# One attention and expert kernel: k in tiles of four blocks, with the scores at a tile's first block as two products

## The chip, the cores and the metric

The kernel runs on one core of one Trainium2 chip. What counts is the time of one execution on the device, in microseconds (us). Each kernel is run several times; the median is shown, with the lowest and the highest. One more execution is taken with the hardware profiler, and all rows come from it.

## What is computed

Windowed attention over 8 batches, 8 heads, 576 positions and a head size of 64, in f32, and behind it a mixture of 8 experts with one expert for each token. The output of the attention, (4608, 512), is the tokens of the second part. The change lies in the scores of the first part.

```python
scores = scale * np.matmul(q, k.transpose(0, 1, 3, 2))
rel = pos[:, None] - pos[None, :]
mask = (rel >= 0) & (rel < window)            # window = 64
scores = np.where(mask, scores, -1000000000.0)
attn = np.exp(scores - max); attn = attn / (sum(attn) + 1e-09)
out = np.matmul(attn, v)
...
do_compute = (x @ w_skip) > 0; e_idx = argmax(xc @ w_gate)
h = np.maximum(xc[mask] @ w1[e], 0.0)
y[mask] = gate_w[mask, None] * (h @ w2[e]);  out[do_compute] = xc + y
```

A position sees itself and the 63 before it. With blocks of 64 positions (9 for each batch), a block of queries therefore needs two blocks of keys: its own and the one before it.

## The kernel before

**Tiles.** A tile is 128 tokens: two blocks of 64, one in each half of the partitions. `token_tiles` gives 36 of them in four rounds m of 9: four tiles for each of the two batches of a round (blocks 0 to 7), and a tail tile, r = 8, with block 8 of both batches. PE's array is used in four parts of 64x64: hf, the half of the tile (which block), picks the columns and r, one of two heads, the rows. p runs over the four pairs of heads.

**Loads.** q, k and v come in groups n = 2b + g of four blocks (g is the half of a batch, NG = 16). `load_qk` (L203) loads q and k of a group, `load_v` (L309) vT and vm of it: vT feeds the gate's product (`gate`, L332, product pw at L336), vm the product av (L388). `load_qk_tail` (L213) and `load_v_tail` load block 8 for a round. k has four fixed tiles of five blocks, `ks` (L198): slot 0 of a tile is a copy of the block before the tile's first. For a first half (g = 0) there is none, and slot 0 of the tiles 0 and 2 is set to zero once, by two memsets on POOL (L200). For a second half (g = 1) the load takes five blocks of kT, the last of the first half among them. A tail load takes two blocks of each batch's kT, 7 and 8. So every window of two blocks of keys lies side by side, and `windows` (L222) gives each half of a tile one piece of 128 columns.

**Scores.** `score(t)` (L231) writes the mask into the PSUM tile ps with four products of 512 columns (the band, L238), and adds 16 products of q with 128 columns of k (L252). The mask has -2^36 in every masked place; for block 0 the whole first half is masked. Then DVE subtracts the row maximum, ACT takes the exponent, PE transposes (pt, L285), ACT copies, PE multiplies with v (av, L388), DVE divides, and SP stores.

**Order.** All is written by hand under `tc.manual_schedule()`: each engine's queue has the order of the code. In iteration t of the loop at L1144 come the loads that are due (`at`: q and k five tiles ahead of their first use, v four), then score(t + 1), gate products, softmax of t, av of t - 2, the transposes of t - 1. The loads stand on SP's queue, only the first ones also on ACT's. SP's transfers use eight semaphores in turn (DMAHW0 to 7): each waits until the transfer eight before it has landed, beside what its own buffer needs. A pool gives out the buffer that came free first.

After tile 35 come the last routing steps and the experts, whose weights SP loads from L833 on. Neither is touched.

Of the kernel before, what the change touches and what calls it, by code (L numbers as in the profile page):

```python
# [8 lines left out]
F32 = mybir.dt.float32  # L9
# [11 lines left out]
P = 128  # L21
# [24 lines left out]
LAT = 320  # L46
ROUND = 1.5 * 2.0**23

NQB, NKB, NVB, NTB, NSB, NPB, XPB = 4, 4, 4, 2, 2, 3, 4

AHEADQ, AHEADV = 5, 4
SDELAY = 2
# [21 lines left out]
def token_tiles():  # L74
    tiles = []
    for b in range(B):
        for j in range(4):
            tiles.append(((b, 2 * j), (b, 2 * j + 1)))
        if b % 2 == 1:
            tiles.append(((b - 1, 8), (b, 8)))  # L80
    return tiles
# [62 lines left out]
def window_attention_moe(ctx: ExitStack, tc, a, out):  # L144
    nc = tc.nc
    tiles = token_tiles()
# [47 lines left out]
    qkp = scoring.enter_context(tc.tile_pool(name="qkp", bufs=1))  # L194


    NG = 2 * B
    ks = [qkp.tile([P, 5, 4, 64], F32, name=f"k{s}") for s in range(NKB)]  # L198
    for k in ks[::2]:
        nc.gpsimd.memset(k[:, 0], 0.0)  # L200
    qs, tails = {}, {}

    def load_qk(n, parts=((0, 4),), other=nc.sync):  # L203
        b, g = divmod(n, 2)
        if parts[0][0] == 0:
            qs[n] = qkp.tile([P, 4, 4, 64], F32, name="q", bufs=NQB)
        q, k = qs[n], ks[n % NKB]
        for s, e in parts:
            s0 = s + 1 if s or not g else 0
            nc.sync.dma_start(k[:, s0 : e + 1], a["kT"][b, :, 4 * g + s0 - 1 : 4 * g + e])  # L210
            other.dma_start(q[:, s:e], a["qT"][b, :, 4 * g + s : 4 * g + e])

    def load_qk_tail(m):  # L213

        q = qkp.tile([P, 2, 4, 64], F32, name="qt")
        k = qkp.tile([P, 2, 2, 4, 64], F32, name="kt")
        for z in range(2):
            nc.sync.dma_start(k[:, z], a["kT"][2 * m + z, :, 7:9])
            nc.sync.dma_start(q[:, z], a["qT"][2 * m + z, :, 8])
        tails[m] = q, k  # L220

    def windows(t):  # L222

        m, r = divmod(t, 9)
        if r == 8:
            q, k = tails[m]
            return [(q[:, z], k[:, z]) for z in range(2)]
        n, j = 4 * m + r // 2, 2 * (r % 2)
        return [(qs[n][:, j + z], ks[n % NKB][:, j + z : j + z + 2]) for z in range(2)]

    def score(t):  # L231

        ps = psc.tile([P, 2, 4, P], F32, name="ps")
        kinds = [min(i, 1) for _, i in tiles[t]]
        for hf in range(2):
            for r in range(2):
                h = slice(64 * r, 64 * r + 64)
                nc.tensor.matmul(  # L238
                    ps[64 * hf : 64 * hf + 64, r],
                    identb[h, h],  # L240
                    band[h, kinds[hf]].unsqueeze(1).to_broadcast([64, 4, P]),
                    start=True,
                    stop=False,
                    skip_group_check=True,
                )
        win = windows(t)
        for p in range(4):
            for hf in range(2):
                for r in range(2):
                    h = slice(64 * r, 64 * r + 64)  # L250
                    q, k = win[hf]
                    nc.tensor.matmul(  # L252
                        ps[64 * hf : 64 * hf + 64, r, p],
                        q[h, p],
                        k[h, :, p],
                        start=False,
                        stop=p == 3,
                        skip_group_check=True,
                    )
        ss[t] = ps  # L260

    def soften(t):
# [841 lines left out]
    with tc.manual_schedule():  # L1104
        other = nc.scalar
        nc.sync.dma_start(identb, a["c_identb"])
        other.dma_start(band, a["c_band"])
        load_qk(0, ((0, 1),), other)
        load_qk(0, ((1, 2),), other)
        load_qk(0, ((2, 4),), other)  # L1110
        load_vT(0)
        other.dma_start(wg, a["wg"])
# [6 lines left out]
        at = {}  # L1119
# [16 lines left out]
        for m in range(B // 2):  # L1136
            when_at(9 * m + 4, load_qk_tail, m)
            when_at(9 * m + 2, load_v_tail, m)
            lower_at.setdefault(9 * m + 4, []).append((tail_lower, m, 0))
            lower_at.setdefault(9 * m + 7, []).append((tail_lower, m, 1))  # L1140
            gate_at.setdefault(9 * m + 5, []).append((gate_tail, m))
            gate_at.setdefault(9 * m + 6, []).append((gate_tail_t, m))
        score(0)
        for t in range(NT - 1):  # L1144
            m, r = divmod(t, 9)
            for f, n in at.get(t, ()):
                f(n)
            score(t + 1)
            gates = gate_at.get(t, ())
            if t > 1:  # L1150
# [200 lines left out]
        while True:  # L1351
            k = place[0]
            i, qi = steps[min(k, len(steps) - 1)]
# [14 lines left out]
    with tc.For_i(0, more, 1) as i:  # L1368
# [3 lines left out]
        at = mr.tile([P, NT], I32, name="atl")  # L1372
# [11 lines left out]
        for qi in range(NQ):  # L1384
            both = []
            for w in range(2):
                n = 2 * qi + w
# [56 lines left out]
```

## Time and profile before

| | us |
|---|---|
| median of 3 runs | 423.96 |
| lowest, highest | 423.83, 426.25 |
| the profiled execution's time | 421.13 |
| its span in the trace | 419.4 |
| PE busy | 397.0 |
| DVE busy | 292.0 |
| ACT busy | 220.1 |
| POOL busy | 159.3 |

The trace is that of the profiled execution alone, so rows are held against its 421.13 us, and what is worked out there is carried over to the median. PE is TensorE's products, PEld its weight loads, DVE VectorE, ACT ScalarE, POOL GpSimd, SP the queue that issues most transfers. An f32 product of the program is two rows of the profile. Busy time of PE counts from a product's start to its modelled end, and products overlap: where a row gives a stretch and a count, the time from its start to the start of the next row is what it took of PE.

### The profile page before, as it was taken

Reading aid. Unit: us, or ns where it says so; the run is one execution under the profiler, and the core shown is the slowest. Engines: PE = TensorE matmul, PEld = TensorE weight load, DVE = VectorE, ACT = ScalarE, POOL = GpSimd, SP = SyncE. Lnnn points to the kernel's source line nnn. Section 1 sums busy time; section 2 is a strip of 40 time slices with the busy share of each in tenths; the row PEclk is TensorE's granted clock in tenths of the full one; section 3 lists DMA queues with packets and bytes.
Section 4 is the critical chain, followed back from the end, with each engine's and each line's share of the span. In section 5 each row is a group of like instructions: output and inputs, shape, how many; then the busy total and the mean of one; then the engine's idle time right before and its main releaser. Section 6 shows DMA issues by size and latency. Waiting matters only on the chain.

```text
span 419.4 us, 11769 instructions
## 1 busy us (share of the span) xinstructions
PE 397.0 (95%) x4673; PEld 333.4 (80%) x4673; DVE 292.0 (70%) x513; ACT 220.1 (52%) x388; POOL 159.3 (38%) x298
## 2 busy tenths in 40 slices
PE   5998999999999989889999999999999999999992
PEld 3666878888778778679988898898888889988881
DVE  2596799989799797999437679555556485656561
ACT  0775777777767685536224436234335345544530
POOL 5211148756958878576203105013016030101011
PEclk9999899999999999999999999999999999999997
DMA  8999999999996596546928937545388765767800
GB/s 264 406 339 337 402 379 346 408 413 310 364 412 228 148 357 215 185 160 184 333 72 274 304 121 246 193 157 204 129 269 267 263 203 193 239 196 233 280 33 21
DMA packets 38840, 105.71 MB, mean 252 GB/s; under 512 B 4896, under 2 KB 6816, under 8 KB 38784
## 3 DMA queue, kind: packets, MB, share of 16 engines
q1 hardware_dynamic: 34160, 93.51, 65.2%
q0 software_dynamic: 3200, 9.58, 6.5%
q10 hardware_dynamic: 1424, 1.85, 1.2%
q8 instruction: 37, 0.61, 0.6%
q14 instruction: 19, 0.16, 0.1%
HBM read 90.86 MB, written 14.39 MB: 251 GB/s over the span
## 4 chain that ended last, share of the span: by engine, by line
PE 73%; DMA 9%; DVE 6%; POOL 5%; ACT 3%; issue 2%; ACTq 0%; DVEq 0%; POOLq 0%
PE p L910 9%; PE p L912 8%; PE p L911 8%; PE av L388 6%; PE pt L285 5%; PE ps L252 4%; PE yv L910 4%; PE yv L911 4%; PE yv L912 4%; DMA vTt<-vTt 3%; PE yw L910 3%; PE yw L912 3%; PE yw L911 3%; DMA k<-kT 2%; PE px L887 2%
## 5 line engine op out<-in xcount | busy, mean ns | idle before, releaser
L846 DVE TENSOR_TENSOR wlo<-raw,whi 128x1024 fp32r<-128x1024 f32 x70 | 86.9, 1253 | 17.5 <-ACT whi L842 17.4
L956 ACT ACTIVATE hh<-p 128x256 fp32r<-128x256 f32 (+6 forms) x72 | 27.7, 385 | 127.0 <-PE p L912 126.3
L910 PE MATMUL p<-xh,whi 128*128 128x256 f32 (+6 forms) x288 | 85.4, 296 | 0.2 <-DVE hl L959 0.2
L912 PE MATMUL p<-xh,wlo 128*128 128x256 f32 (+6 forms) x288 | 83.7, 291 | 0.6 <-DVE wlo L846 0.6
L911 PE MATMUL p<-xl,whi 128*128 128x256 f32 (+6 forms) x288 | 83.5, 290 | 0.0
L842 ACT CAST whi<-raw 128x1024 fp32r<-128x1024 f32 x72 | 74.3, 1046 | 0.1
L994 POOL DMA_INDIRECT out<-yo,les x18 | 17.6, 976 | 146.7 <-DVE yo L993 144.2
L959 DVE SCALAR_TENSOR_TENSOR hl<-p,hh 128x256 fp32r<-128x256 f32 (+6 forms) x72 | 30.2, 420 | 60.7 <-ACT hh L956 35.0
L910 PEld LDWEIGHTS p<-xh,whi 128*128 128x128 f32 x288 | 54.5, 189 | 3.8 <-issue 1.7
L911 PEld LDWEIGHTS p<-xl,whi 128*128 128x128 f32 x288 | 54.6, 190 | 1.0
L912 PEld LDWEIGHTS p<-xh,wlo 128*128 128x128 f32 x288 | 54.6, 190 | 0.8 <-DVE wlo L846 0.8
L271 DVE TENSOR_REDUCE mx<-ps 128x8 f32<-128x1024 f32 x36 | 43.6, 1212 | 9.7 <-PE ps L252 9.7
L277 ACT ACTIVATE s<-s 128x1024 f32<-128x1024 f32 x36 | 38.1, 1059 | 22.3 <-DVE s L272 22.2
L272 DVE TENSOR_TENSOR s<-ps,mx 128x1024 f32<-128x1024 f32 x36 | 44.1, 1225 | 5.0 <-ACT vm L364 0.5
L388 PEld LDWEIGHTS av<-vm,ptm 128*64 128x64 f32 x992 | 35.0, 137 | 10.9 <-issue 3.9
L388 PE MATMUL av<-vm,ptm 128*64 128x74 f32 x992 | 40.0, 232 | 2.0 <-ACT ptm L286 1.1
L286 ACT COPY ptm<-pt 128x512 f32<-128x512 f32 x72 | 38.3, 582 | 5.4 <-PE pt L285 5.4
L285 PE MATMUL pt<-ident,s 128*128 128x128 f32 x288 | 40.0, 283 | 0.0
L252 PE MATMUL ps<-k,q 64*64 64x128 f32 x1024 | 36.9, 280 | 2.6 <-DMA q<-qT 1.7
L252 PEld LDWEIGHTS ps<-k,q 64*64 64x64 f32 x1024 | 32.1, 139 | 7.0 <-issue 3.2
L285 PEld LDWEIGHTS pt<-ident,s 128*128 128x128 f32 x288 | 31.6, 143 | 2.5 <-issue 0.2
L357 POOL COPY vm<-vm 64x1184 f32<-64x1184 f32 x16 | 18.7, 1167 | 33.8 <-ACT vm L356 31.0
(224 smaller groups left out, 695.8 us busy)
## 6 DMA issues: line engine op xcount, KB each, us to landing
raw<-wq SPq DMA_DIRECT2D x72, 512.0 KB, 4.9
vm<-vp SPq DMA_DIRECT2D x15, 592.0 KB, 9.1
vT<-vT SPq DMA_DIRECT2D x16, 512.0 KB, 7.5
out<-x SPq DMA_DIRECT2D x32, 256.0 KB, 7.3
q<-qT SPq DMA_DIRECT2D x14, 512.0 KB, 8.8
wr<-wq SPq DMA_DIRECT2D x24, 256.0 KB, 5.7
k<-kT SPq DMA_DIRECT2D x7, 640.0 KB, 8.4
k<-kT SPq DMA_DIRECT2D x7, 512.0 KB, 8.5
```

The costliest lines, as they stand in the source:

```text
L252: nc.tensor.matmul(ps[64 * hf : 64 * hf + 64, r, p], q[h, p], k[h, :, p], start=False, stop=p == 3, skip_group_check=True,)
L271: nc.vector.tensor_reduce(mx, flat, axis=AX.X, op=ALU.max)
L272: pace[0] = nc.vector.tensor_tensor(s, flat, mx.unsqueeze(2).to_broadcast([P, 8, P]), op=ALU.subtract)
L277: nc.scalar.activation(s, s, AF.Exp, scale=0.125)
L285: nc.tensor.transpose(pt[:, p], s[:, 4 * r + p], ident)
L286: nc.scalar.copy(ptm[:, 4 * r : 4 * r + 4], pt)
L388: nc.tensor.matmul(av[64 * hf : 64 * hf + 64, h // 4, (h % 4) * VW : (h % 4 + 1) * VW], ptm[:, (h % 2) * 4 + h // 2, 64 * hf : 64 * hf + 6 ...
L842: nc.scalar.copy(ring[n % RING][0], raws[n % NRAW])
L846: by.tensor_tensor(lo, raws[n % NRAW], hi.bitcast(F32), op=ALU.subtract)
L910: nc.tensor.matmul(o, lh, rh, start=first, stop=False)
L911: nc.tensor.matmul(o, lh, rl, start=False, stop=False)
L912: nc.tensor.matmul(o, ll, rh, start=False, stop=last)
```

## The change

k of a group lies in a tile of four blocks of its own, from a pool with five buffers, as q's does. The block in front is not loaded again and nothing is set to zero. `windows` now answers for one half of a tile and gives pieces: for a block inside a group one piece of 128 columns, as before; for block 4 (the first of a second half) and block 8 (the tail) two pieces of 64, the first from the tile of the group before; for block 0 one piece of 64 columns, its own block. `score` runs over p, then the pieces z, then the halves, then r. A tail load takes block 8 of k for both batches, then of q.

```diff
--- before.py
+++ after.py
@@ -46,7 +46,7 @@
 LAT = 320
 ROUND = 1.5 * 2.0**23
 
-NQB, NKB, NVB, NTB, NSB, NPB, XPB = 4, 4, 4, 2, 2, 3, 4
+NQB, NKB, NVB, NTB, NSB, NPB, XPB = 4, 5, 4, 2, 2, 3, 4
 
 AHEADQ, AHEADV = 5, 4
 SDELAY = 2
@@ -195,38 +195,39 @@
 
 
     NG = 2 * B
-    ks = [qkp.tile([P, 5, 4, 64], F32, name=f"k{s}") for s in range(NKB)]
-    for k in ks[::2]:
-        nc.gpsimd.memset(k[:, 0], 0.0)
-    qs, tails = {}, {}
+    qs, ks, tails = {}, {}, {}
 
     def load_qk(n, parts=((0, 4),), other=nc.sync):
         b, g = divmod(n, 2)
         if parts[0][0] == 0:
             qs[n] = qkp.tile([P, 4, 4, 64], F32, name="q", bufs=NQB)
-        q, k = qs[n], ks[n % NKB]
+            ks[n] = qkp.tile([P, 4, 4, 64], F32, name="k", bufs=NKB)
         for s, e in parts:
-            s0 = s + 1 if s or not g else 0
-            nc.sync.dma_start(k[:, s0 : e + 1], a["kT"][b, :, 4 * g + s0 - 1 : 4 * g + e])
-            other.dma_start(q[:, s:e], a["qT"][b, :, 4 * g + s : 4 * g + e])
+            nc.sync.dma_start(ks[n][:, s:e], a["kT"][b, :, 4 * g + s : 4 * g + e])
+            other.dma_start(qs[n][:, s:e], a["qT"][b, :, 4 * g + s : 4 * g + e])
 
     def load_qk_tail(m):
 
-        q = qkp.tile([P, 2, 4, 64], F32, name="qt")
-        k = qkp.tile([P, 2, 2, 4, 64], F32, name="kt")
-        for z in range(2):
-            nc.sync.dma_start(k[:, z], a["kT"][2 * m + z, :, 7:9])
-            nc.sync.dma_start(q[:, z], a["qT"][2 * m + z, :, 8])
-        tails[m] = q, k
-
-    def windows(t):
+        tails[m] = [qkp.tile([P, 2, 4, 64], F32, name=f"{x}t") for x in "kq"]
+        for x, z in zip("kq", tails[m]):
+            for hf in range(2):
+                nc.sync.dma_start(z[:, hf], a[x + "T"][2 * m + hf, :, 8])
+
+    def windows(t, hf):
 
         m, r = divmod(t, 9)
+        b, i = tiles[t][hf]
         if r == 8:
-            q, k = tails[m]
-            return [(q[:, z], k[:, z]) for z in range(2)]
-        n, j = 4 * m + r // 2, 2 * (r % 2)
-        return [(qs[n][:, j + z], ks[n % NKB][:, j + z : j + z + 2]) for z in range(2)]
+            k, q = tails[m]
+            return q[:, hf], [(ks[2 * b + 1][:, 3:4], 0), (k[:, hf : hf + 1], 64)]
+        n, j = 2 * b + i // 4, i % 4
+        k = ks[n]
+        if j:
+            win = [(k[:, j - 1 : j + 1], 0)]
+        else:
+            win = [(ks[n - 1][:, 3:4], 0)] if i else []
+            win.append((k[:, 0:1], 64))
+        return qs[n][:, j], win
 
     def score(t):
 
@@ -243,20 +244,22 @@
                     stop=False,
                     skip_group_check=True,
                 )
-        win = windows(t)
+        win = [windows(t, hf) for hf in range(2)]
         for p in range(4):
-            for hf in range(2):
-                for r in range(2):
-                    h = slice(64 * r, 64 * r + 64)
-                    q, k = win[hf]
-                    nc.tensor.matmul(
-                        ps[64 * hf : 64 * hf + 64, r, p],
-                        q[h, p],
-                        k[h, :, p],
-                        start=False,
-                        stop=p == 3,
-                        skip_group_check=True,
-                    )
+            for z in range(2):
+                for hf in range(2):
+                    q, parts = win[hf]
+                    for k, at in parts[z : z + 1]:
+                        for r in range(2):
+                            h = slice(64 * r, 64 * r + 64)
+                            nc.tensor.matmul(
+                                ps[64 * hf : 64 * hf + 64, r, p, at : at + 64 * k.shape[1]],
+                                q[h, p],
+                                k[h, :, p],
+                                start=False,
+                                stop=p == 3,
+                                skip_group_check=True,
+                            )
         ss[t] = ps
 
     def soften(t):
```

What stands in the queues now is told by the built programs, one row for instructions of one kind that follow each other (x is their number; here a product is one instruction). PE, score(2), the tile of blocks 4 and 5 of batch 0. Before, with the band's products ahead of it:

```order
41 L238 MATMUL ps<-band,identb 64x512
42 L238 LDWEIGHTS identb
43 L238 MATMUL ps<-band,identb 64x512
44 L252 MATMUL ps<-k_107,q 64x128 x16
45 L285 MATMUL pt<-ident,s 128x128 x8
```

And with the change, at the same place:

```order
51 L255 MATMUL ps<-k,q 64x64 x2
52 L255 MATMUL ps<-k,q 64x128 x2
53 L255 MATMUL ps<-k,q 64x64 x4
54 L255 MATMUL ps<-k,q 64x128 x2
55 L255 MATMUL ps<-k,q 64x64 x4
56 L255 MATMUL ps<-k,q 64x128 x2
57 L255 MATMUL ps<-k,q 64x64 x4
58 L255 MATMUL ps<-k,q 64x128 x2
59 L255 MATMUL ps<-k,q 64x64 x2
60 L288 MATMUL pt<-ident,s 128x128 x8
```

16 products became 24: for each p two narrow ones of block 4's first piece, two wide ones of block 5, two narrow ones of block 4's second piece. The rows around it stand as before.

PE, score(8), the first tail tile. Before it was one row of 16 products as well; with the change:

```order
148 L255 MATMUL ps<-k,qt 64x64 x4
149 L255 MATMUL ps<-kt,qt 64x64 x4
150 L255 MATMUL ps<-k,qt 64x64 x4
151 L255 MATMUL ps<-kt,qt 64x64 x4
152 L255 MATMUL ps<-k,qt 64x64 x4
153 L255 MATMUL ps<-kt,qt 64x64 x4
154 L255 MATMUL ps<-k,qt 64x64 x4
155 L255 MATMUL ps<-kt,qt 64x64 x4
156 L339 MATMUL pw<-vT,wg 32x256 x4
```

16 products of 128 columns became 32 of 64, half of them on the second halves' k and half on the tail's own.

SP, from the load of k for group 4 to that of vm for group 4 (the sizes are elements for each partition). Before:

```order
21 L210 DMA k_106<-kT 128x1024
22 L211 DMA q<-qT 128x1024
23 L218 DMA kt<-kT 128x512
24 L219 DMA qt<-qT 128x256
25 L218 DMA kt<-kT 128x512
26 L219 DMA qt<-qT 128x256
27 L426 DMA out<-x 128x512
28 L296 DMA vT<-vT 128x1024
29 L302 DMA vm<-vp 128x2x592
```

With the change:

```order
20 L206 DMA k<-kT 128x1024
21 L207 DMA q<-qT 128x1024
22 L214 DMA kt<-kT 128x256 x2
23 L214 DMA qt<-qT 128x256 x2
24 L429 DMA out<-x 128x512
25 L299 DMA vT<-vT 128x1024
26 L305 DMA vm<-vp 128x2x592
```

The number of transfers is the same, so each keeps its place in the turn of eight; the two loads of kt stand together and are half as large. Everywhere else on SP only sizes differ. On POOL the two memsets of k are gone; the order of DVE and ACT is the same.

## Rows read from the trace of the kernel before

**Rows 1.** The page's first section: busy us (share of the span) x instructions.

```profile
PE 397.0 (95%) x4673; PEld 333.4 (80%) x4673; DVE 292.0 (70%) x513; ACT 220.1 (52%) x388; POOL 159.3 (38%) x298
```

**Rows 2.** The page's shares of the chain that ended last, by engine.

```profile
PE 73%; DMA 9%; DVE 6%; POOL 5%; ACT 3%; issue 2%; ACTq 0%; DVEq 0%; POOLq 0%
```

**Rows 3.** The waits of PE: engine, product, line, cause; total us, times, longest.

```profile
PE ps L252 <- DMA q<-qT: 1.7, 2, 1.2
...
PE av L388 <- POOL vm L357: 0.8, 1, 0.8
PE ps L252 <- issue: 0.8, 1, 0.8
```

**Rows 4.** The chain that ended last, in order of time: start us, us, what.

```profile
18.42 13.09 DMA vTt<-vTt
...
34.00 7.13 DMA vT<-vT
```

**Rows 5.** Timeline of PE: start us, stretch us, line, product, shape, count [wait before].

```profile
31.64 0.42 PE L336 MATMUL pw<-vTt,wg 128*32 128x128 f32 x8 [0.98 <-DMA vTt<-vTt]
...
38.35 1.04 PE L252 MATMUL ps<-kt,qt 64*64 64x128 f32 x32
41.26 0.64 PE L336 MATMUL pw<-vT,wg 128*32 128x256 f32 x8 [1.87 <-DMA vT<-vT]
41.83 1.67 PE L388 MATMUL av<-vm,ptm 128*64 128x74 f32 x32
43.43 1.97 PE L285 MATMUL pt<-ident,s 128*128 128x128 f32 x8
45.33 0.64 PE L238 MATMUL ps<-band,identb 64*64 64x512 bf16 x4
45.75 1.12 PE L252 MATMUL ps<-k,q 64*64 64x128 f32 x32
...
57.16 0.41 PE L238 MATMUL ps<-band,identb 64*64 64x512 bf16 x4
57.40 1.04 PE L252 MATMUL ps<-k,q 64*64 64x128 f32 x32
58.38 0.64 PE L336 MATMUL pw<-vT,wg 128*32 128x256 f32 x8
58.95 1.25 PE L388 MATMUL av<-vm,ptm 128*64 128x74 f32 x32
60.13 1.10 PE L285 MATMUL pt<-ident,s 128*128 128x128 f32 x8
61.16 0.41 PE L238 MATMUL ps<-band,identb 64*64 64x512 bf16 x4
```

**Rows 6.** Windows: stretch, its us, engines busy (x), granted clock, DMA share, GB/s.

```profile
31.64:41.26 9.62, 7.75 (x163) 6.43 (x164) 6.18 (x13) 5.93 (x11) 1.92 (x5) 1.00 0.98 336
39.39:41.26 1.87, 0.00 (x1) 0.03 (x1) 1.74 (x4) 0.57 (x1) 0.00 (x0) 1.00 1.05 365
42.48:45.90 3.42, 3.42 (x36) 2.75 (x35) 2.29 (x5) 1.99 (x3) 0.00 (x0) 0.50 1.01 400
45.33:57.16 11.83, 11.83 (x241) 9.48 (x240) 9.79 (x17) 8.54 (x14) 4.46 (x6) 0.98 1.03 408
```

**Rows 7.** Transfers issued up to 45 us: queue, count, KB each, median us to landing.

```profile
k<-kT SPq DMA_DIRECT2D x2, 640.0 KB, 8.8
...
kt<-kT SPq DMA_DIRECT2D x2, 256.0 KB, 6.0
```

**Rows 8.** Windows of L252 alone, inside one score: PE and PEld busy (x running).

```profile
57.40:57.42 0.02, 0.02 (x4) 0.02 (x4) 1.00 1.93 768
57.42:57.51 0.09, 0.09 (x4) 0.09 (x4) 1.00 1.06 421
57.51:57.53 0.02, 0.02 (x8) 0.02 (x8) 1.00 0.27 102
```

**Rows 9.** Timeline of PE, the end of score(0) and the start of score(1).

```profile
6.69 0.64 PE L238 MATMUL ps<-band,identb 64*64 64x512 bf16 x2
6.89 0.42 PE L252 MATMUL ps<-k,q 64*64 64x128 f32 x2
```

## The prediction

> **What bounds the kernel now.** The page's first section says which engine to follow: PE is busy for 397.0 of 419.4 us [rows 1]. The shares of the chain that ended last say the same: PE 73%, and transfers 9% [rows 2]. So something that shortens transfers can only pay inside those 9%, and something that lengthens PE pays nearly everywhere. Next the waits of PE: 1.7 us for q at the start, 0.8 us for POOL, and 0.8 us put down to "issue" [rows 3]; the two waits for v stand in the timeline of PE, 0.98 us ahead of 31.64 and 1.87 us ahead of 41.26 [rows 5]. After 41.26 PE waits for no transfer in the attention stage.
>
> The chain in order of time shows where the 9% are: 13.09 us of the load of vTt from 18.42, and 7.13 us of the load of vT (group 4) from 34.00 to 41.13 [rows 4]. The windows agree: the 16 DMA engines are at a share of 0.98 to 1.05 there, and move 336 to 408 GB/s [rows 6]. The first 41 us are thus a stream of bytes that PE waits for; from 41 us to the end of the attention stage PE runs from one product to the next, with few waits [rows 3]. A tile is then 4.00 us of PE (57.16 to 61.16), of which the scores are 0.98 us, 57.40 to 58.38 [rows 5].
>
> [...]
>
> **The change, part by part.** *Fewer bytes.* A second-half load of k falls from 640 to 512 KB, a tail load of k from 256 to 128 KB [rows 7]. Over the kernel that is 16 times 128 KB. Ahead of the vT load that PE waits for at 41.26 stand the second half of batch 0 (its first part falls from 384 to 256 KB), that of batch 1, and two tail loads: 4 x 128 KB = 0.524 MB. At 408 to 336 GB/s [rows 6] that is 1.28 to 1.56 us; I take 1.3. Half of it stands ahead of vTt, so the 0.98 us wait falls to about 0.3, PE comes to the second wait some 0.65 us sooner, and its 1.87 us fall to about 1.2. Together **-1.3 us**.
>
> *The clock.* [...] Start to start: av 41.83 to 43.43 = 1.60 against 58.95 to 60.13 = 1.18; the transposes 43.43 to 45.33 = 1.90 against 60.13 to 61.16 = 1.03; the band 45.33 to 45.75 = 0.42 against 57.16 to 57.40 = 0.24 [rows 5]. The sum of the differences is 0.42 + 0.87 + 0.18 = 1.47 us. The clock fell after a wait of 1.87 us and not after those of 0.98 and 0.8 us [rows 3, 5]. With 1.2 us to go I am nearer to the latter, and take it as gone: **-1.47 us**; the other end is 0.
>
> *More products.* Block 4 of each batch (8 tiles) has 8 products more, each tail tile (4 of them) 16; the profile shows every f32 product as two rows (16 products are its x32), so 16 and 32 rows. Block 0 has as many as before, half as wide. Tiles 2, 6 and 8 lie in front of the wait at 41.26, which hides them. 9 tiles remain: 11, 15, 20, 24, 29, 33 and the tails 17, 26, 35. The trace has no f32 product of 64 columns on a 64x64 part of the array, so its price is bounded. Far end: each row costs its share of a score, 0.98/32 = 0.031 us, whatever its columns; 6 x 16 + 3 x 32 = 192 rows are 5.9 us. Near end: only columns count. The rows speak for it: the four parts of the array work beside each other, four products start within 0.02 us and the next four 0.11 us later [rows 8]. A split leaves each part as many columns as before, so the cost is 0. What could be short is the weight load of each narrow product, which must fit into a half round, 0.055 us. The nearest row is av: its 32 rows have 64 weight columns too, 74 moved ones, go two beside each other, and take 1.18 us, that is 16 rounds of 0.074 with the start [rows 5]. A tail of 16 rounds at that price is 1.18 instead of 0.98 us, +0.2. I take a quarter of it, since 64 columns are fewer than 74 and a start is in it: 0.05 x 9 = **+0.45 us** (0 to 1.8; far 5.9).
>
> [...]
>
> *What costs nothing.* The two memsets of k on POOL go; the first products wait 1.7 us for q anyway [rows 3]. The order of SP's queue is the same but for kt and qt, and no load of k gains a wait for PE: it waits for the transfer eight before it, as ever. Block 3 of a second half is now held until the tail tile; the fifth buffer covers that, since the pool gives out the buffer that came free first. If it did not, a load would stand behind a tile of 4.00 us, five tiles ahead of its use. Some 512 rows of PE more must be fetched; the "issue" wait of 0.8 us stands once [rows 3], and one more would cost 0.8. I take 0.
>
> **The sum.** The profiled execution took 421.13 us, 419.4 of it span. 421.13 - 1.3 - 1.47 + 0.45 = 418.8, that is -2.3 us. What is gained at 41 us is kept as far as PE goes on from product to product; where POOL, DVE and ACT end last, late in the stage, they work on what PE hands them, and the one wait of PE for POOL is 0.8 us [rows 3]. The profiled execution lies 2.8 us under the median of the runs, 423.96; the same difference there gives 421.6.
>
> **The rivals.**
> 1. *The clock falls all the same.* For it: 1.2 us lies between the waits with and without a fall. -1.3 + 0.45 = -0.85: 423.1.
> 2. *The timed runs lose more here than the profiled one.* They are 2.8 us slower, by something the profile doesn't show; were it further waits of PE at the same transfers, and went with them: -2.3 - 2.8: 418.9. Against it: nothing shows where the 2.8 us are.
> 3. *Every row costs the same, wide or narrow* (0.031 us). [...] -2.77 + 5.9 = +3.1: 427.1.
> 4. *The overlap breaks* (the slower side). In a block-4 tile two parts of the array get four narrow products while the others get two wide ones; if the rows of a score then went one behind the other, at 0.12 us a wide one (0.98/8) and 0.06 a narrow one, a score would take 32 x 0.06 + 16 x 0.12, or 64 x 0.06: 3.8 instead of 0.98 us. 9 x 2.9 - 2.77 = +23: 447. It decides from 7.0/9 = 0.8 us per tile on (4.24 us, 1% of the median, and the 2.77 gained). Against it: at 6.69 us products of the next tile's band start ahead of two of the tile before, at 6.89 [rows 9], so one part does not hold up another.
> 5. *The bytes were hidden anyway*, the load at 41.13 being late for a reason that 0.5 MB do not touch: then only +0.45 remains, 424.4. Against it: the share of 0.98 [rows 6].
>
> [...]
>
> **How the numbers follow.** Chances: the forecast 0.52, rival 1 0.16, rival 2 0.12, rival 3 0.09, rival 4 0.05, rival 5 0.06. The forecast's own range is 420.9 (-1.56 - 1.47, and splits that cost nothing) to 423.0 (splits at 1.8). From 418.5 to 425.5 lie the forecast and rivals 1, 2 and 5, 0.86 of the chance; rivals 3 and 4 are left out. About 1% is what a measurement of this kernel can tell from no change. Below 419.7 lies rival 2, and the forecast with the spread of the runs (423.83 to 426.25) in its favour, 0.12 + 0.06 = 0.18; above 428.2 rival 4 and the edge of rival 3, 0.07; within 1% the rest, 0.75.
>
> **What the changed profile would show.** Bytes: the wait ahead of the products of vT near 41 us at about 1.2 us, and the gate starting near 40.0 instead of 41.26. Clock: no stretch at 0.50 after it, and the tile after it in 4.0 us. Products: a tail score of 64 rows in 1.0 to 1.1 us; 1.9 would be rival 3, 3.8 rival 4. SP: no load of k that waits for PE. The prediction is wrong if PE waits somewhere else for what it gained, above all for vT or vm of the groups after, which would then come later than PE wants them.

## The result and the profile after

| | before | after |
|---|---|---|
| median of 15 runs each, us | 424.69 | 427.38 |
| lowest, highest | 422.12, 427.88 | 425.45, 429.78 |
| span of the profiled execution | 419.4 | 426.1 |
| ratio of after to before | | 1.0073, 95% interval 1.0053 to 1.0093 |
| PE busy | 397.0 | 399.3 |

The forecast was 421.6 us with a range from 418.5 to 425.5. The change made the kernel slower, by about 3 us, and the median after lies outside the range. In a second pair of profiles the spans are 422.2 (before) and 425.5 (after); the 6.7 us between the first two are explained below.

The page of the profile after, its first section and the shares of the chain, against [rows 1, 2]:

```profile
PE 399.3 (94%) x4929; PEld 336.3 (79%) x4929; DVE 291.2 (68%) x513; ACT 220.3 (52%) x388; POOL 158.2 (37%) x296
PE 80%; POOL 6%; DVE 5%; issue 4%; DMA 3%; ACT 2%; ACTq 0%; POOLq 0%; DVEq 0%
```

Transfers fell from 9% of the chain to 3%, and "issue" rose from 2% to 4%. So what was to go did go, and something else came. The waits of PE say what (the line, for whom, the sum in us, how many, the longest), against [rows 3]:

```profile
PE av L391 <- issue: 5.1, 5, 1.5
PE ps L239 <- DMA band<-c_band: 2.9, 1, 2.9
PE ps L255 <- DMA q<-qT: 1.7, 2, 1.1
PE lp L563 <- POOL xg L614: 1.7, 1, 1.7
PE ps L255 <- issue: 1.4, 3, 0.7
PE pw L339 <- issue: 0.3, 1, 0.3
```

Before there was one wait on "issue", 0.8 us. Now there are nine, 6.8 us. The waits for vT and vTt are gone from the list altogether. The timeline of PE at the place of [rows 5] (start, duration, what, and in brackets the wait ahead of it) shows both:

```profile
30.43 0.40 PE L339 MATMUL pw<-vTt,wg 128*32 128x128 f32 x8
30.76 0.47 PE L391 MATMUL av<-vm,ptm 128*64 128x74 f32 x7
32.52 1.00 PE L391 MATMUL av<-vm,ptm 128*64 128x74 f32 x25 [1.29 <-issue]
...
39.65 0.64 PE L339 MATMUL pw<-vT,wg 128*32 128x256 f32 x8
40.22 1.26 PE L391 MATMUL av<-vm,ptm 128*64 128x74 f32 x32
```

vTt and vT are there when PE comes (30.43, 39.65). But 7 products into av, in the middle of a run of 32 equal ones that have all they need, PE stands still for 1.29 us. The stretch whose granted clock was 0.50 before [rows 6] is at 1.00:

```profile
42.00:46.00 4.00, 4.00 (x80) 3.15 (x78) 3.49 (x6) 3.44 (x7) 1.17 (x1) 1.00 1.03 408
```

The granted clock is the 1.00 near the end of the row; before, the same four microseconds have 0.57. So the steps on bytes and on the clock came as written, in this profile. And the narrow scores:

```profile
51.31 1.09 PE L255 MATMUL ps<-k,q 64*64 64x64 f32 x48
52.34 0.44 PE L347 MATMUL pk<-ident,vw 128*128 128x128 f32 x2
...
38.62 0.28 PE L255 MATMUL ps<-k,qt 64*64 64x64 f32 x8
...
39.65 0.64 PE L339 MATMUL pw<-vT,wg 128*32 128x256 f32 x8
```

A block-4 score takes 1.03 us from its start to the start of what follows (51.31 to 52.34), and so does a tail score with twice the rows of before (38.62 to 39.65), against 0.98. That is the 0.05 us of the forecast.

Where do the new waits stand? The windows from one wait's end to the next (length, then busy time and number of rows of PE's products, then of its weight loads) count what PE did between them:

```profile
core 0: us, PE busy (x) PEld busy (x) DVE busy (x) ACT busy (x) POOL busy (x), PEclk, DMA share, GB/s
32.52:49.90 17.38, 17.04 (x381) 13.68 (x381) 14.22 (x24) 12.15 (x23) 3.68 (x7) 1.00 1.02 374
49.90:63.34 13.44, 12.26 (x255) 9.67 (x254) 10.92 (x20) 9.12 (x16) 7.02 (x17) 1.00 1.04 374
63.34:75.97 12.64, 11.79 (x254) 9.42 (x255) 10.94 (x21) 8.53 (x18) 9.56 (x26) 1.00 0.98 354
75.97:82.16 6.18, 4.65 (x127) 3.70 (x127) 3.56 (x6) 4.21 (x6) 3.97 (x4) 1.00 1.03 412
82.16:117.38 35.22, 34.55 (x763) 28.12 (x763) 30.08 (x58) 25.06 (x45) 23.16 (x49) 1.00 0.93 320
117.38:135.12 17.75, 17.42 (x382) 13.90 (x381) 16.21 (x32) 12.02 (x21) 11.97 (x45) 1.00 0.87 306
```

762, 509, 509, 254, 1526 and 763 rows: 3, 2, 2, 1, 6 and 3 times 254. PE's trace has 6, 3, 3, 2, 10 and 5 semaphore instructions in these stretches, which the row counts leave out; with them it is 256 each time (768, 512, 512, 256, 1536 and 768). PE waits where its own program passes into another block of 256 instructions. Nothing of data, tiles or heads repeats in that step, and the waits cut runs of equal products in two; that speaks for the program itself being late. The longest wait at such a border is 1.53 us in this profile.

The trace shows the blocks themselves. The packets of one queue of instructions (number, MB, share of the time of 16 DMA engines), before and after:

```profile
q8 instruction: 37, 0.61, 0.6%
q8 instruction: 39, 0.64, 0.6%
```

512 rows more are two packets more (with all scores narrow, in experiment 6, 1,536 more are six), which is one packet for 256 rows, and each packet has 16,384 bytes. In the profile after, such a packet lands 1.2 to 1.5 us ahead of the end of each wait at a border: the wait of 1.53 us ends at 82.16, its packet ran from 79.82 to 80.81. Behind each of these waits the next packet begins only after PE has gone on, by 1.2 to 3.8 us. So PE does wait for its program.

That holds for seven of the nine waits, 6.1 us in all (5.2 us in seven in the second profile of after). The other two stand in the score of the last tail tile, three and a half blocks behind the wait that ends at 135.13, and no packet lands just ahead of them:

```profile
156.02 0.31 PE L255 MATMUL ps<-k,qt 64*64 64x64 f32 x3 [0.33 <-issue]
156.76 0.29 PE L255 MATMUL ps<-k,qt 64*64 64x64 f32 x2 [0.44 <-issue]
```

That score takes 2.44 us from start to start (2.41 in the second profile) instead of 0.97; why stays open.

### The profile page after: what moved, and what is told of

It is laid out like the page before. It is cut to its first block, busy times and chain, and to the rows that moved or that the text cites. A ratio compares the mean times of both kernels' runs of the same rounds, so it can differ in the third digit from the quotient of the medians.

```text
span 426.1 us, 12262 instructions
## 1 busy us (share of the span) xinstructions
PE 399.3 (94%) x4929; PEld 336.3 (79%) x4929; DVE 291.2 (68%) x513; ACT 220.3 (52%) x388; POOL 158.2 (37%) x296
## 4 chain that ended last, share of the span: by engine, by line
PE 80%; POOL 6%; DVE 5%; issue 4%; DMA 3%; ACT 2%; ACTq 0%; POOLq 0%; DVEq 0%
PE p L913 9%; PE p L915 9%; PE p L914 8%; PE av L391 8%; PE pt L288 7%; PE ps L255 6%; PE yv L913 4%; PE yv L914 3%; PE yv L915 3%; PE yw L913 3%; PE yw L914 3%; PE yw L915 3%; PE ps L239 2%; PE pw L339 2%; PE px L890 2%
## 5 line engine op out<-in xcount | busy, mean ns | idle before, releaser
L288 PE MATMUL pt<-ident,s 128*128 128x128 f32 x288 | 39.1, 279 | 0.0
L255 PE MATMUL ps<-k,q 64*64 64x128 f32 (+1 forms) x1152 | 36.9, 260 | 2.0 <-DMA q<-qT 1.7
L255 PEld LDWEIGHTS ps<-k,q 64*64 64x64 f32 x1152 | 33.3, 138 | 5.9 <-DMA q<-qT 3.2
L360 POOL COPY vm<-vm 64x1184 f32<-64x1184 f32 x16 | 18.7, 1167 | 35.4 <-ACT vm L359 31.2
```

The costliest lines, as they stand in the source:

```text
L255: nc.tensor.matmul(ps[64 * hf : 64 * hf + 64, r, p, at : at + 64 * k.shape[1]], q[h, p], k[h, :, p], start=False, stop=p == 3, skip_group_ ...
L288: nc.tensor.transpose(pt[:, p], s[:, 4 * r + p], ident)
```

## The experiments

In all tables "issue" is the sum of all waits of PE on "issue" in the run's own profile, also of the few that stand at no border, and "stage" the end of the last product av. A border is where a new block of 256 rows begins. Each ratio is to runs of before taken together with it, whose median lay between 420.4 and 424.1 us from one set to another.

**1. Both kernels again.** Is the pattern that of the kernel or of one execution?

> The kernel before once more, a second profile of it. Theory F (fetch): PE runs dry at the border of a block of 256 rows when the block is consumed before the next has come, and the first profile (one such wait, 0.79 us) was a fortunate one, since the timed runs are 2.8 us above it: 3 to 5 waits on 'issue', 2 to 4 us in all, a time near 424. Theory R (rows): the waits belong to the changed kernel alone: one wait again, near 421.

> The changed kernel once more, a second profile. If its waits on 'issue' are tied to the place in the program (a block's border against the transfers then under way), the same borders wait again: 6 to 9 waits, 5 to 7 us, time near 427. If they fall by chance, other borders wait, and the sum may be anywhere from 2 to 7 us.

The second profile of before has 3.0 us in three waits on "issue", and no wait for v at 31 or 41 us; that of after has 5.8 us. The timelines, first of before, then of after:

```profile
35.01 0.38 PE L285 MATMUL pt<-ident,s 128*128 128x128 f32 x2 [1.55 <-issue]
42.25 1.25 PE L388 MATMUL av<-vm,ptm 128*64 128x74 f32 x31 [0.98 <-issue]
122.79 0.65 PE L252 MATMUL ps<-k,q 64*64 64x128 f32 x12 [0.42 <-issue]
```

```profile
31.90 1.00 PE L391 MATMUL av<-vm,ptm 128*64 128x74 f32 x25 [0.65 <-issue]
44.17 0.59 PE L255 MATMUL ps<-k,q 64*64 64x128 f32 x10 [1.31 <-issue]
63.48 0.34 PE L391 MATMUL av<-vm,ptm 128*64 128x74 f32 x2 [0.92 <-issue]
81.33 0.48 PE L391 MATMUL av<-vm,ptm 128*64 128x74 f32 x9 [1.63 <-issue]
```

The changed kernel waits at the same product in both profiles (x25 near 32, x2 near 63, x9 near 82 us), and at others in one of them only. So the border decides where, and chance whether. Before has such waits too, but after 43 us nearly none; theory R (none at all before) is too strong.

This profile also shows where the 2.8 us come from by which the first one lay under the median. The windows at 230 us, first profile of before, then the second, with two lines of the second's waits:

```profile
230.00:245.00 15.00, 15.00 (x119) 13.48 (x118) 7.87 (x16) 6.38 (x13) 2.00 (x3) 1.00 0.83 274
```

```profile
230.00:245.00 15.00, 13.14 (x93) 11.32 (x91) 6.47 (x12) 4.82 (x10) 1.38 (x2) 0.89 0.83 263
PE p L910 <- ACT xh L888: 0.9, 1, 0.9
PE p L911 <- DVE xl L891: 0.9, 1, 0.9
```

In the experts, two waits of some 0.9 us (0.7 to 1.0) with a stretch at a lower clock stand in the second profile of before and in both of after, and not in the first. From 164 us to the end the first profile takes 254.9 us, the second 257.9, after 257.9. Of the 6.7 us between the first two profiles, 3.0 are thus not the change's.

**2. The halves of the change.** The bytes alone, and the products alone. In the first the tail loads leave out block 7 of k as well, and DVE sets the zeros.

```diff
-            s0 = s + 1 if s or not g else 0
+            s0 = s + 1
```

> The kernel before, with the blocks in front left out of every load of k (zeros stand there, set once), and products and rows as before: the saved 2 MB alone; it leaves out the keys of the block before at blocks 4 and 8. Forecast's step: -1.3 for the bytes and -1.5 for the clock, so ratio 0.993 to 0.994, no stretch at 0.50. Theory F with pace as the cause (blocks consumed without the pauses at 31 and 41 us find the next block not there): the gain is given back, 4 to 8 waits on 'issue', ratio 0.999 to 1.005. Theory R: no more waits on 'issue' than before, ratio 0.993.

```diff
-        return [(qs[n][:, j + z], ks[n % NKB][:, j + z : j + z + 2]) for z in range(2)]
+            if j + z:
+                win = [(k[:, j + z : j + z + 2], 0)]
+            else:
+                win = [(k[:, 0:1], 0)] if n % 2 else []
+                win.append((k[:, 1:2], 64))
```

> The kernel before with its own loads, but the products at blocks 4, 8 and 0 narrow, as in the changed kernel: 256 more rows of products and as many of weight loads, no byte less. Forecast's step: +0.45 us, ratio 1.001. Theory R (more rows make more waits at block borders): 1.008 to 1.015, 5 or more waits on 'issue' here too, and the pauses for v at 31 and 41 us as before. Theory F with pace as the cause: between, 1.001 to 1.006.

| | ratio | issue, us | stage, us |
|---|---|---|---|
| before, first and second profile | | 0.8, 3.0 | 164.5, 164.3 |
| bytes alone | 0.9988 (0.9963 to 1.0014) | 0.5 | 163.7 |
| products alone | 1.0134 (1.0075 to 1.0194) | 7.4 | 173.0 |
| after, first and second profile | 1.0073 | 6.8, 5.8 | 168.2, 167.3 |

The products do the harm, bytes or no bytes. The fewer bytes bring 0.5 us instead of 1.3 + 1.5; the interval holds no change, and also the 1.3 by itself (at most 1.6). The longest wait of all profiles so far is here, and the clock falls behind it:

```profile
85.23 0.61 PE L399 MATMUL av<-vm,ptm 128*64 128x74 f32 x13 [2.56 <-issue]
85.30:89.00 3.70, 3.70 (x51) 3.10 (x52) 2.91 (x6) 1.85 (x3) 0.00 (x0) 0.59 0.69 207
```

The tail score of tile 17, 64 narrow products and 64 loads in 1.03 us, ends 4 us ahead of the row behind the wait. So theory R, as put for this run, has the sign and the size: more rows, more waits, whatever the loads.

**3. Rows without work, and fewer bytes beside the same rows.** The masks in sixteen products instead of four have the same columns, but 864 rows more. In this form, as where q is not loaded, the scores come out as other numbers and tokens go to other experts; only the attention stage is compared.

```diff
+        for p in range(4):
-                    ps[64 * hf : 64 * hf + 64, r],
-                    band[h, kinds[hf]].unsqueeze(1).to_broadcast([64, 4, P]),
+                    ps[64 * hf : 64 * hf + 64, r, p],
+                    band[h, kinds[hf]],
```

> The kernel before with its own loads and scores, but the four products of 512 columns of each mask as sixteen of 128: as many columns, 12 products and 12 weight loads more in each of the 36 tiles, 864 rows, 3.4 blocks. If rows cost only what they take of the array: ratio 0.999 to 1.003. If PE is held by the fetch (some 6 us for 256 rows while the transfers are saturated, 188 rows a tile, so 4.4 us instead of 4.0 in about 20 tiles): +6 to +12 us, ratio 1.015 to 1.03, with waits on 'issue' at most borders from 32 to 118 us.

```diff
-            qs[n] = qkp.tile([P, 4, 4, 64], F32, name="q", bufs=NQB)
+            qs[n] = qs[n - 4] if n >= 4 else qkp.tile([P, 4, 4, 64], F32, name="q", bufs=NQB)
...
-            other.dma_start(qs[n][:, s:e], a["qT"][b, :, 4 * g + s : 4 * g + e])
+            if n < 4:
+                other.dma_start(qs[n][:, s:e], a["qT"][b, :, 4 * g + s : 4 * g + e])
```

> The changed kernel with q loaded for the first four groups only (the others use those four again, so their scores are other numbers): 12 loads of 512 KB less, the same rows on PE. Theory F: with the engines of the transfers less full, the waits on 'issue' from 46 to 118 us (3.5 to 5 us in the two profiles of the changed kernel) go, ratio 0.990 to 0.997. Theory S: they stay, ratio 1.004 to 1.010.

The sixteen products take 0.25 us, from 64.02 to 64.27, where four took 0.24 (57.16 to 57.40 in [rows 5]):

```profile
64.02 0.42 PE L239 MATMUL ps<-band,identb 64*64 64x128 bf16 x16
64.27 1.05 PE L253 MATMUL ps<-k,q 64*64 64x128 f32 x32
```

And yet the stage ends at 170.1 us, 5.8 us later than in the second profile of before, with 4.9 us of waits on "issue". Rows that cost the array 0.01 us a tile cost the stage 5.8 us, a little under the +6 to +12 expected. It is not a fixed time for each block: six blocks pass between 57 and 91 us, at 5.7 us each, with a single wait of 0.2 us.

With 6 MB of q less, the waits on "issue" from 46 to 118 us fall from 4.5 and 3.2 us (the two profiles of after) to 1.4, and the stage ends at 162.9 us. The rows of PE are the same, which speaks for a part of the queue of transfers: theory F, not theory S (the fetch is slow by itself). It is one profile, though, and theory F had the waits gone. Both kernels have their long waits where the DMA engines are at a share of about 1 (1.00 to 1.06 in the 6 or 7 us ahead).

**4. Fewer transfers at a time.** Each transfer of SP's queue also waits for the fourth (or sixth) before it.

```diff
+            i = start(*x, **y)
+            if len(under) >= DEPTH:
+                tc.add_manual_dep(i.ins, under[-DEPTH].ins.name, info)
+            under.append(i)
```

> The changed kernel, with at most four of SP's transfers under way in the attention stage instead of eight: each load or store there also waits for the fourth before it. Theory F (a block of 256 rows of PE's program is fetched behind the transfers that are queued, 6 to 7 us with eight under way, and a block lasts PE 5.4 to 6.2 us): the fetch gets shorter, the waits on 'issue' at block borders go from about 6 us to under 2, ratio to the kernel before 0.992 to 0.998. Theory S (the fetch is slow by itself, whatever else is queued): the same 6 us of waits, ratio 1.006 to 1.010, or worse where a load comes late.

> The kernel before with the same limit of four. Theory F: its two or three waits on 'issue' (2.5 us in the second profile) go, ratio 0.993 to 0.998. Theory S: 0.999 to 1.002.

> The changed kernel with at most six transfers of SP under way instead of eight, up to tile 28. Theory F: the fetch waits shorten by about a quarter of 6 us each, so the waits on 'issue' fall from 6 us to 1 or 2, and data waits stay under 2 us: ratio 0.996 to 1.003. If data comes late as with four: 1.01 to 1.02.

| at most | kernel | ratio | issue, us | stage, us |
|---|---|---|---|---|
| 4 | after | 1.0422 (1.0366 to 1.0478) | 0 | 181.5 |
| 4 | before | 1.0434 (1.0395 to 1.0474) | 0 | 182.8 |
| 6, to tile 28 | after | 1.0057 (1.0024 to 1.0091) | 4.1 | 167.7 |

With four, not one wait on "issue" is left in either kernel. But the data comes late instead, for PE and, behind the stores, for DVE; the page of after with four:

```profile
PE pw L340 <- DMA vT<-vT: 8.8, 5, 4.0
PE av L392 <- DVE lh L411: 4.7, 3, 2.5
PE ps L256 <- DMA q<-qT: 3.0, 3, 1.4
```

The ratio that theory F gave (0.992 to 0.998) is far off: I had counted what the shorter fetch gives and not what the limit itself costs: in after with four, SP waited for the transfer four before, 30.2 us in sum where that was a load of vm and 20.2 where it was one of vT, and DVE waited 18.7 us for stores to land, which it does not do in after.

That no wait on "issue" is left does not by itself prove the mechanism, since a PE that waits for data also gives the fetch time. The packets of the program show more. From 32 to 118 us they begin, on the mean, 2.8 and 2.9 us (after, both profiles) and 2.9 and 3.0 us (before) behind the border before them; with four transfers under way 1.8 us (after) and 1.5 us (before). With q not loaded it is 2.4 us. These are estimates, since the time of a border without a wait is worked out from the counted rows. With six it is 3.1 us: the waits on "issue" fall by a third there, which is worth less than the noise, but the packets do not begin sooner.

**5. Which rows, and where the borders fall.** One kind of narrow score at a time, and all borders moved by 128 rows, with 72 short products in place of the 8 long ones in the first tile.

```diff
-            return q[:, hf], [(ks[2 * b + 1][:, 3:4], 0), (k[:, hf : hf + 1], 64)]
+            return q[:, hf, 0], [(k[:, hf], 0)]
```

> The changed kernel, but a tail load takes blocks 7 and 8 of k again (128 KB more each, 1 MB in all) and the tail scores are 16 products of 128 columns: only block 4 stays narrow. If the waits come from blocks that narrow products use up faster (the block with a tail score lasts PE 4.65 to 5.1 us instead of 5.7 to 6.4): the borders behind a tail (rows 1473, 3009 and 4545 of the changed kernel) wait no longer, some 2.5 of 6 us of waits go, ratio 1.001 to 1.004. If it is the number of rows in all: half of the added rows stay, half the loss, 1.003 to 1.005.

```diff
+            return [(q[:, z], [(k[:, z, 0:1], 0), (k[:, z, 1:2], 64)]) for z in range(2)]
```

> The kernel before with its own loads, but the tail scores as two products of 64 columns (and block 0 as one): 128 rows of products and as many weight loads more, in four tiles. If the waits come from blocks that are used up faster: waits on 'issue' behind the tails, 2 to 4 us in all, ratio 1.003 to 1.008. If they come from block 4 or from the loads of the changed kernel: ratio 0.999 to 1.002.

```diff
-        for _ in range(n):
+        for _ in range(9 * n):
-                idle[:, 0], identb, band[:, 0].unsqueeze(1).to_broadcast([P, 4, P]),
+                idle[:32, 0, :56], identb[:, :32], band[:, 0, :56],
```

> The changed kernel with 72 short products instead of the 8 long ones that keep PE busy in the first tile: 128 rows more, so that every border of a block falls 128 rows earlier in the work. Theory F: the waits on 'issue' stand again 256 rows apart, at the same remainder of the count from the start as before, that is at other places of the work; the tail of tile 17 then lies across a border and the 1.5 us behind it shrinks; the sum of waits 3 to 6 us, ratio 1.002 to 1.008. If the waits belong to the work (the products behind a narrow score): they stand at the same products, 128 rows further in the count.

> The kernel before with the same 72 short products: 128 rows more. Theory F: waits on 'issue' at the same remainder of the count, 1 to 4 us in all, ratio 0.998 to 1.006: where the borders fall is worth a few us by itself. If rows only count where they crowd: no change, 0.999 to 1.001.

| | ratio | issue, us | stage, us |
|---|---|---|---|
| after, tails wide | 1.0016 (0.9992 to 1.0041) | 2.5 | 164.5 |
| before, tails narrow | 1.0050 (1.0024 to 1.0077) | 3.0 | 168.0 |
| after, borders moved | 1.0052 (1.0020 to 1.0084) | 3.1 | 166.2 |
| before, borders moved | 0.9988 (0.9959 to 1.0017) | 0.3 | 165.0 |

The four tails are a third of the tiles that change and have half of the added rows. With wide tails what remains can't be told from no change, and narrow tails alone cost 0.5%; but both intervals also hold half of the loss, so it is not shown that rows in a tail cost more than others. A tail passes its 128 rows of products and loads within 1 us. With before's loads and narrow tails PE waits in the middle of the tail of tile 17, after 28 of 64 rows:

```profile
77.85 0.63 PE L262 MATMUL ps<-kt,qt 64*64 64x64 f32 x28
80.06 0.80 PE L262 MATMUL ps<-kt,qt 64*64 64x64 f32 x36 [1.58 <-issue]
```

With 128 rows ahead, the waits of after stand at other products:

```profile
35.87 0.44 PE L255 MATMUL ps<-k,q 64*64 64x128 f32 x5 [0.70 <-issue]
41.80 1.18 PE L391 MATMUL av<-vm,ptm 128*64 128x74 f32 x29 [0.69 <-issue]
54.70 1.25 PE L391 MATMUL av<-vt,ptm 128*64 128x74 f32 x31 [1.06 <-issue]
83.87 0.99 PE L391 MATMUL av<-vm,ptm 128*64 128x74 f32 x24 [0.60 <-issue]
```

Counted from the start they are again at the same remainder of 256, and the 1.5 us at x9 near 82 us, behind the tail of tile 17, is gone. So the waits belong to the count, not to the products.

**6. All scores narrow, and bytes without rows.**

```diff
-            win = [(k[:, j - 1 : j + 1], 0)]
+            win = [(k[:, j - 1 : j], 0), (k[:, j : j + 1], 64)]
```

> The changed kernel with every score in products of 64 columns: 32 more products and 32 more weight loads in each tile that has none split, 16 and 16 in the 8 tiles with block 4 and in the 4 with block 0; some 1,500 rows, 6 blocks. If PE is held by the fetch of its rows: a tile of 4.0 us has 228 rows instead of 164, a block lasts 4.5 us where its fetch takes 5.8 to 7.2, so 1.2 us more in each of some 20 tiles, +15 to +25 us against the changed kernel, ratio to the kernel before 1.04 to 1.065, with a wait at nearly every border from 32 to 118 us. If narrow products cost only their 0.05 us a tile (the forecast's step): +1.3 us, ratio 1.01.

The ratio is 1.0462 (1.0406 to 1.0518), the waits on "issue" 14.6 us, and the stage ends at 183.1 us, 14.9 later than in after. The rows, of PE's timeline, of its waits, and of the clock behind a wait:

```profile
56.52 1.10 PE L255 MATMUL ps<-k,q 64*64 64x64 f32 x64
57.56 0.64 PE L339 MATMUL pw<-vT,wg 128*32 128x256 f32 x8
PE ps L255 <- issue: 10.3, 8, 2.4
44.00:48.00 4.00, 4.00 (x44) 3.61 (x45) 1.03 (x4) 1.84 (x5) 1.17 (x1) 0.58 1.05 417
```

A score with all rows narrow takes 1.04 us (56.52 to 57.56) against 0.98. In the 16 tiles that have no narrow score in after, and a part of it in the 16 others with block 0 or 4, this is some 1.5 us. The waits are 7.8 us more than in after. Three stretches of 4 us with a granted clock of 0.58, 0.58 and 0.57 on the mean lose some 1.7 us each. Together 14.4 of 14.9, as an estimate. A wait at every border, as expected, it is not: there is one after every one to five blocks, and blocks of 4.1 to 4.8 us pass in between.

Last, the bytes saved with no row added: the nine blocks of a batch side by side in one tile, three such tiles, and q in three buffers.

```diff
-    ks = [qkp.tile([P, 5, 4, 64], F32, name=f"k{s}") for s in range(NKB)]
+    ks = [qkp.tile([P, 9, 4, 64], F32, name=f"k{s}") for s in range(NKB)]
-        return [(qs[n][:, j + z], ks[n % NKB][:, j + z : j + z + 2]) for z in range(2)]
+        k, i = ks[n // 2 % NKB], 4 * (n % 2) + j
+        return [(qs[n][:, j + z], k[:, max(i + z - 1, 0) : i + z + 1]) for z in range(2)]
```

> Bytes saved and no narrow product: the nine blocks of a batch's k lie side by side in one of three tiles, so that every window of 128 columns is whole; q has three buffers instead of four, for the room. Rows on PE as in the kernel before, bytes as in the changed one. Theory F: waits on 'issue' as in the kernel before (1 to 3 us), the waits for v at 31 and 41 us shorter, ratio 0.995 to 1.000. If q's third buffer holds up SP's queue: 1.00 to 1.01.

> The same with at most six transfers under way up to tile 28. Theory F: no wait on 'issue' left, ratio 0.992 to 0.998 unless data comes late in its place, as with four: 1.01.

Its ratio is 0.9965 (0.9939 to 0.9991): 1.5 us faster than before, and faster than the changed kernel. It has 1.8 us of waits on "issue", and still waits 0.9 us each for vTt and vT. With at most six transfers it has none on "issue", but waits 2.0 us for vT, and the ratio is 1.0008 (0.9981 to 1.0035). The exchange of experiment 4 is seen again: fewer transfers under way take off waits for the program, and the data comes later.

## Why the prediction was wrong

**The step that failed** is the one at the end of "What costs nothing": 512 rows of PE more must be fetched, the "issue" wait of 0.8 us stands once, "one more would cost 0.8. I take 0." The row was read, and its price was right (0.2 to 1.6 us each); wrong was to count on none. At borders after has seven waits in each profile, 6.1 and 5.2 us, against one of 0.8 and three of 3.0 us in the two of before: 2.2 to 5.3 us more. I had asked only whether the rows fit the array, and not whether the program's blocks, which narrow products use up faster, come fast enough while the data's transfers fill the DMA engines. A look at which instruction of L252 the one wait of before stood ahead of would have been a start: it too cuts a run of equal products in two, and lies at a border of 256.

**Bytes, -1.3.** The mechanism is as put: PE starts the products of vTt and vT 1.2 and 1.6 us sooner in after (30.43 against 31.64, 39.65 against 41.26) and doesn't wait for them. The size in the timed runs stays open. Bytes alone gave -0.5 us (0.9988, at most 1.6), and without added rows and with another layout of k -1.5 (0.9965, 0.4 to 2.6); both intervals hold 1.3, and neither holds 1.3 + 1.47. In the second profile of before the two waits for v are not there either: 1.55 and 0.98 us for the program stand in the same place. There a shorter wait for v has nothing to give. The prediction also read the chain too narrowly: the two loads that it names are 20.2 us, some half of the 9% of transfers.

**The clock, -1.47.** The fall behind 41 us, to 0.50 [rows 6], in which most of the longer times that the term compares lie, belongs to the first profile. After has none there (1.00 from 42 to 46 us), but neither has the second profile of before (1.00 from 34 to 46 us), in which PE waits 0.98 us instead of 1.87. One of two profiles had nothing to gain, so a fall seen once was no ground for the whole term. The opposite is seen where waits grow: after 2.34 and 2.56 us the granted clock was 0.58 and 0.59 for some 4 us.

**Narrow products, +0.45.** Right where the score has no wait in it: 1.03 instead of 0.98 us. The tails of tiles 26 and 35 take longer (2.03 and 2.44 us in the first profile), the one cut by a border, the other for the open reason above.

**The sum** in its own terms, from the first profile of before to that of after, to the end of the stage (164.5 to 168.2, +3.7): -2.9 for both waits for v, -1.5 for the clock, +0.4 for narrow scores, +5.3 for the program, +1.5 for the last tail score. That is +2.8 of 3.7. The waits for ACT, DVE and POOL change little in sum (1.07 instead of 0.29 us for ACT at one product, but one of 1.1 us at another is gone), and the rest I have not followed. The other 3.0 us of 6.7 lie in the experts and are the first profile's own.

**The rivals.** Rival 3 had the time (427.1; measured 427.38) by luck, for the wrong reason: four narrow rows do run beside each other, as the score of 1.03 us shows; what costs is not a row on the array but a block of rows to be brought. Rival 2 was half right: in the second profile of before, 2.9 us slower than the first, the difference is no wait at the transfers but lies in the experts, and the change doesn't touch it. Rivals 1 and 4 are not seen in the profiles of after. Rival 5 isn't either, as the products of vTt and vT start sooner, but the timed runs of the bytes alone can't exclude it.

**What stays open.** The packets tell when a block came: PE waits at a border where the packet begins late or the block before is short. By the counted rows, the packets of the two kernels begin 0.9 to 5.3 us behind the border before them (32 to 118 us, four profiles); the packet before the wait of 1.53 us began 3.8 us behind it and took 1.0 us, PE went on 1.4 us after it had landed, and PE had used up its block in 4.7 us. No view shows when a block was asked for, so why one packet begins sooner than another is not told. That the queue of data transfers delays them rests on the limit of four (1.5 and 1.8 us instead of 2.8 to 3.0) and, less cleanly, on the 12 loads left out; the limit of six doesn't show it. Open too is what holds up the last tail score.

## What to carry to other kernels

Splitting a product costs instructions even where it costs the array next to nothing (0.25 us for sixteen products against 0.24 for four): before doing so, look whether the engine shows waits on "issue", whether they lie a whole number of blocks of 256 rows apart, and whether the DMA engines are full in that stage; if all three hold, each added row is to be priced, here at 5 to 7 us of waits for 500 to 900 rows. The packets of the instruction queue, against the times at which PE passes the borders, tell whether a wait is one for the program. Saving a second copy of data is better done by a layout in which the pieces lie side by side than by more and smaller products. And one profile of a kernel is one draw: take a second before a wait of a microsecond, or a fall of the clock, is entered as something to be gained.

## What was not expected of the hardware

- PE stood still for up to 2.56 us in the middle of equal products, at distances of 254 counted rows (256 with the semaphore instructions) or a multiple. In the profile after the DMA engines were at a share of 0.99 to 1.05 in the 6 or 7 us ahead of each such wait but one, of 0.33 us, where it was 0.73. At such borders it went on 1.1 to 1.8 us after a packet of 16,384 bytes had landed on the instruction queue, in every run with such a wait.
- Sixteen products of 128 columns took 0.25 us and four of 512 columns 0.24, and 64 narrow rows 1.04 us against 0.98 for 32 wide ones.
- The granted clock fell to 0.50 behind a wait of 1.87 us for data, and for the program to 0.58 and 0.59 (means over some 4 us) behind 2.34 and 2.56 us. Behind 1.53 us it did not, and behind one of 2.18 us, with all scores narrow, it did not either.
